# An mLSTM cell and a squared-relu FFN in one kernel: weight roundings moved one place ahead, one relu moved ahead of a conversion, four filler matmuls left out

## The chip, the core and the metric

The kernel runs on one core of one Trainium2 chip. The core has a matrix engine (PE, with its own weight-load row, PEld), a vector engine (DVE), a scalar engine (ACT), a general engine (POOL), and a queue (SP) that here only issues DMAs. Each engine runs its own list of instructions strictly in order; semaphores tie the lists together. The metric is the device time of one execution in microseconds, as the median of several runs; lower is better. Before the change five runs gave 519.08, 521.13, 518.82, 519.87 and 517.87 us, median 519.08.

## What is computed

```python
# attention: per batch and head, over 768 steps t, head_dim 40
m_new  = max(f[t] + m, i[t])
C      = exp(f[t] + m - m_new) * C + exp(i[t] - m_new) * outer(v[t], k[t])
n      = exp(f[t] + m - m_new) * n + exp(i[t] - m_new) * k[t]
y[t]   = sigmoid(o[t]) * (C @ q[t]) / max(abs(n @ q[t]), 1)
# the 8 heads side by side give x: 3072 rows of 320
h      = max(x @ w_in, 0)          # w_in  320 x 2048
out    = (h * h) @ w_out           # w_out 2048 x 320
```

All of it in fp32. The weights w_in and w_out reach the chip as pairs of 32-bit words (64-bit floats) and are turned into fp32 by the kernel itself.

## The kernel before, in words

**Tiles.** The 3072 rows of x are 24 row blocks of 128 (block s). The cell is worked in chunks: inside a block by matrix products of scores, between blocks by the carried state C. For each block: `transposes(s)` turns k and q on PE, ACT copies them out; `scores(s)` multiplies them; `weigh(s)` makes the decay weights W on ACT from the gate rows A_bc, which POOL masks first (`mask`); `weighted(s)` multiplies scores by W on DVE (tile P_sb); `attend(s)` makes three groups of matmuls, hi (from the state), dC (the state's increment) and hp (from P_sb); DVE takes them out of PSUM (num at line 466, C_sb at 471, the sum at 589); `normalise(s)` makes x_sb with six short DVE instructions (lines 595 to 603); `turn_rows(s)` turns x_sb on PE, and ACT copies it to xT. Two blocks make a group of 256 rows for the FFN: `ffn1(g, pp)` is a quarter of the first product (sixteen matmul instructions at line 649 and eight at 660 in the profile), `relu_half` the relu of a quarter on ACT (line 675, two instructions), `square_half` the squares on DVE (line 682).

**Weights.** A list of 26 pieces is rounded by class `Rounding`: pieces 0 to 9 are w_in (512 columns each), 10 to 25 are w_out (320 columns each). One piece n passes four stages: `fetch` (DMA on SP into one of four raw buffers), `words` (ACT lines 195 and 197, tiles mag and low, three buffers each), `join` (DVE lines 206, 210 and 211, then POOL line 215, which writes the fp32 weight), and `join` ends by fetching the piece four places further on, because its raw buffer is now read. `step` makes the words that are missing, usually those of one piece ahead as well, and one join. The first quarter of ffn1 needs pieces 0 to 2, the second 0 to 4, the third 0 to 7, the fourth 0 to 9.

**Order.** The order is written out by hand, and each engine takes its instructions in that order. A prologue (lines 815 to 876) treats blocks 0 and 1, with one `rounding.join()` at line 839 and three steps later on (858, 867, 876). Then a loop of eight parts, u = 0 to 7 (line 880), treats blocks 2 to 5: even parts make scores of block s = 2 + u // 2, odd parts attend to it and turn the next block's k and q; each part makes one quarter of ffn1 (u = 0 to 3: group 0). At the end of part u steps are made until `NEXT[u]` pieces are joined. After the loop a longer list of parts treats the rest, mostly ffn1, ffn2 and the turned form of the attention; its first parts join the last pieces (`LAST`).

**Buffers.** PSUM has three banks for attention products (tag at), taken in rotation by tp, scores, hi, dC and hp, and three for ffn1 (tag h_ps), also taken in rotation; `idle(n)` takes one of these too. `idle(n)` is n bf16 matmuls of zeros, 128x512, whose output nobody reads.

**DMA.** All loads go through SP's queue in program order. [...]

Of the kernel before, what the change touches and what calls it, by code (L numbers as in the profile page):

```python
# [29 lines left out]
def kernel(  # L30
# [200 lines left out]
    rounding = Rounding()  # L231
# [25 lines left out]
    def turn_gates():  # L257
        for src, dst in ((i_sb, b_T), (A_sb, eA_T)):
            tp = ps_o.tile([P, W], F32, name="tp", tag="o_ps")[:, : S // P * BH].rearrange("p (c r) -> p c r", r=BH)
            for c in range(NB):  # L260
                nc.tensor.transpose(tp[:, c, :], src[:, c * P : (c + 1) * P], ident[:BH, :BH])
            nc.scalar.activation(
                dst[:].rearrange("p b c h -> p c b h"), tp.rearrange("p c (b h) -> p c b h", b=B),
                AF.Copy if dst is b_T else AF.Exp,
            )
# [52 lines left out]
    def load_o(s):  # L318
        b, c = divmod(s, NB)
        r, (s0, s1) = next((r, (a, z)) for r, (a, z) in enumerate(RUNS) if a <= s < z)  # L320
        if s == s0:
            st["og", r] = ld.tile([P, 4, H, D], F32, name="og")
        og = st.setdefault(s, {})["og"] = st["og", r][:, s - s0]
        nc.sync.dma_start(og, o_gate[b, :, c * P : (c + 1) * P, :].rearrange("h p d -> p h d"))
# [31 lines left out]
    def mask(s):  # L356

        A = st[s]["A"][0]
        nc.gpsimd.affine_select(  # L359
            A[:], A[:], compare_op=ALU.is_ge, fill=-1e30, base=0, pattern=[[0, H], [1, P]], channel_multiplier=-1,  # L360
        )
# [9 lines left out]
    def weigh(s, masked=False, sums=True):  # L371
        b, c = divmod(s, NB)
        d = st[s]
        A, n = d["A"], H // len(d["A"])
        d["W"] = prep.tile([P, H, P], F32, name="W_sb")
        if s < X_SQ:
            d["dec"] = prep.tile([P, H], F32, name="dec")
        if len(A) == 1 and not masked:
            mask(s)
        for i in range(len(A)):  # L380
            hh = slice(i * n, (i + 1) * n)
            for h in range(n):
                nc.scalar.activation(  # L383
                    d["W"][:, i * n + h, :], A[i][:, h, :], AF.Exp, bias=b_T[:, b, c, i * n + h : i * n + h + 1],
                )
            if s < X_SQ:
                nc.scalar.activation(d["dec"][:, hh], A[i][:, :, P - 1], AF.Exp)
        if sums:
            values(s)

    def values(s):
        b, c = divmod(s, NB)
        d = st[s]
        if c + 1 < NB:
            d["vw"] = prep.tile([P, H, D1], F32, name="vw")
            nc.gpsimd.tensor_tensor(  # L396
                d["vw"][:], d["va"][:], d["W"][:, :, P - 1 : P].to_broadcast([P, H, D1]), op=ALU.mult,
            )
# [5 lines left out]
    def transposes(s, o=(False, False), apart=0):  # L404
        d = st[s]
        kqT(s)
        for i, n in enumerate(("kT", "qT")):
            if i > 0 and apart:
                idle(apart)
            tp = bank(o[i])  # L410
            for j in range(PR):
                nc.tensor.transpose(  # L412
                    tp[:, j, :], d["kq"][:, i, 2 * j : 2 * j + 2, :].rearrange("p h d -> p (h d)"), ident[:],
                )
            (nc.scalar.copy if i == 0 or s in (0, *range(2, 7)) else nc.vector.tensor_copy)(d[n], tp)

    def scores(s, o=(False, False)):
        d = st[s]

        sc = [bank(o[i]) for i in range(2)]  # L420
        for j in range(PR):
            for i in range(2):
                rows = slice(DP * i, DP * i + D)
                nc.tensor.matmul(  # L424
                    sc[i][:, j, :], lhsT=d["kT"][rows, j, :], rhs=d["qT"][rows, j, :], start=True, stop=True,
                )
        d["sc"] = sc

    def weighted(s, spare=False):
        d = st[s]  # L430
        d["P"] = []
        for i in range(2):
            t = ffn.tile([P, W], F32, name="r_sb", bufs=4) if spare else work.tile([P, W], F32, name="P_sb")
            t = t[:].rearrange("p (j t) -> p j t", j=PR)
            d["P"].append(t)
            heads = slice(i, H, 2) if s < KQ_SQ else slice(PR * i, PR * (i + 1))
            nc.vector.tensor_tensor(t, d["sc"][i], d["W"][:, heads, :], op=ALU.mult)  # L437
# [190 lines left out]
    def turn_rows(s):  # L628
        d = st[s]
        t = xT_half(s)  # L630
        tp = ps_at.tile([P, 3, P], F32, name="tp", tag="at")
        for a in range(3):
            nc.tensor.transpose(tp[:, a, :], d["x"][:, a * P : (a + 1) * P], ident[:])
        nc.scalar.copy(t, tp[:])
        del st[s]
# [29 lines left out]
    def ffn1(g, pp):  # L665
        ffn1_main(g, pp)
        ffn1_rest(g, pp, st["half"][0])

    def relu_half():
        if "half" in st:  # L670
            hs, g4 = st.pop("half")
            rs = []
            for h in hs:
                rs.append(ffn.tile([P, 2, WG], F32, name="r_sb", bufs=4))
                nc.scalar.activation(rs[-1][:], h[:], AF.Relu)  # L675
            st.setdefault("relu", []).append((rs, g4))

    def square_half():
        if st.get("relu"):
            rs, g4 = st["relu"].pop(0)  # L680
            for i, r in enumerate(rs):
                nc.vector.tensor_tensor(g4[:, :, i, :], r[:], r[:], op=ALU.mult)  # L682
# [116 lines left out]
    def idle(n):  # L799
        t = ps_h.tile([P, W], F32, name="idle", tag="h_ps")  # L800
        for _ in range(n):
            nc.tensor.matmul(  # L802
                t[:], lhsT=zeros[:, :1].to_broadcast([P, P]), rhs=zeros[:, :1].to_broadcast([P, W]), start=True, stop=True,
            )
# [32 lines left out]
    rounding.words()  # L837
    turn_gates()
    rounding.join()
    weigh(0)  # L840
    transposes(1, (False, True))
    spread_A(1)
# [33 lines left out]
    rounding.step()  # L876


    NEXT = (5, 8, 10, 11, 13, 15, 17, 19)
    for u in range(8):  # L880
        s = 2 + u // 2
        relu_half()
        if u % 2 == 0:
            if u == 0:
                ffn1(0, 0)
                scores(s)
                weighted(s)
                relu_half()
                rounding.step()
            else:  # L890
                if u == 2:
                    idle(4)
                turn_rows(s - 1)
                scores(s)
                ffn1(u // 4, u % 4)
            if u == 2:
                rounding.words()
            if u > 0:
                weighted(s)
            if u == 2:  # L900
                mask(s + 1)
                rounding.join()
                rounding.join()
                weigh(s + 1, masked=True)
                rounding.words()
            elif u == 0:
                rounding.words()
                weigh(s + 1, sums=False)
            else:
                weigh(s + 1)  # L910
                square_half()
        else:
            load_A(s + 2)
            for r in {1: (4,), 3: (5, 6), 5: (7,), 7: ()}[u]:
                load(r)
            if u == 5:
                for r in range(4, 8):
                    sigmoid(r)
            attend(s)
            if u == 3:  # L920
                square_half()
            sum_of_h(s)
            if u < 4:
                normalise(s)
            rounding.join()
            if u == 1:
                values(s + 1)
            if u > 4:
                normalise(s)
            for r in {5: (8,), 7: (9,)}.get(u, ()):  # L930
                load(r)
            for r in {5: (7,), 7: (8,)}.get(u, ()):
                pair_up(r)
            if u > 4:
                load_o(2 * s)
                load_o(2 * s + 1)
            transposes(s + 1)
            rounding.words()
            if u == 7:
                ffn1_main(1, 3)  # L940
                turn_rows(5)
                ffn1_rest(1, 3, st["half"][0])
                square_half()
                relu_half()
            else:
                ffn1(u // 4, u % 4)
                if u > 1:
                    square_half()
        if u < 4:
            load_o(4 + u)  # L950
        while rounding.done < NEXT[u]:
            rounding.step()
        if u == 1:
            square_half()
# [249 lines left out]
```

## Time and profile before

| what | value |
|---|---|
| median of five runs | 519.08 us (517.87 to 521.13) |
| the profiled execution, its own time | 519.08 us, of which the span is 517.3 us |
| PE busy | 509.2 us, 98% of the span |
| DVE busy | 335.4 us, 65%; in the stretch from 40 to 65 us of the span 4.77 to 4.93 us of each 5 |
| ACT, POOL busy | 194.2 us (38%), 91.0 us (18%) |
| granted PE clock | 0.997 as a mean; 1.00 in nearly every stretch, 0.50 from 61 to 64 us |
| PE's busy time from 65 to 120 us | 54.65 of 55 us |

The page gives busy time of each engine, its groups of instructions, and which semaphore ended each idle time; the trace gives the instructions in order of time, and stretches of the span with the busy time and the granted clock in each. The loop of eight parts runs from about 32 us (u = 0) to about 100 us; u = 1 ends at about 47 us on PE, u = 2 at about 55 us, u = 3 at about 68 us.

### The profile page before, as it was taken

The page shows a single profiled execution, that of the slowest core. Times are in us where ns is not written, and L with a number is a line of the kernel's source. Part 1 is how long each engine was busy: PE and PEld are TensorE (multiplying, and loading weights), DVE is VectorE, ACT ScalarE, POOL GpSimd, SP SyncE. Part 2 cuts the span into 40 slices and gives each one's busy share as a digit, 9 for nine tenths or more (in the row PEclk, how much of TensorE's full clock was granted, in tenths as well). Part 3 has the DMA queues.
Part 4 walks back from the last instruction along what each step waited for, and adds up shares of the span by engine and source line. Part 5 has one row for each costly group of instructions (what it writes and reads, how often), then busy time and mean ns, then how long its engine had stood idle before and what let it go on. Part 6 is the DMA issues. An engine that isn't in the chain of part 4 may idle for free.

```text
span 517.3 us, 10367 instructions
## 1 busy us (share of the span) xinstructions
PE 509.2 (98%) x3935; PEld 448.3 (87%) x3937; DVE 335.4 (65%) x638; ACT 194.2 (38%) x460; POOL 91.0 (18%) x110
## 2 busy tenths in 40 slices
PE   9998999999999999999999999999999999999997
PEld 4777788887798898998898898998998998998997
DVE  8479988877894684774864865664864863431461
ACT  3776568534455324432335424135332301103000
POOL 3255643232312120010110110111111000000000
PEclk9999899999999999999999999999999999999999
DMA  9998599976868667868676686686664221200000
GB/s 194 229 208 182 141 186 201 205 173 125 174 154 183 132 158 152 179 119 168 153 148 128 156 153 122 155 144 140 150 148 73 70 67 48 63 1 0 27 27 25
DMA packets 239394, 68.06 MB, mean 132 GB/s; under 512 B 185744, under 2 KB 233872, under 8 KB 239344
## 3 DMA queue, kind: packets, MB, share of 16 engines
q1 hardware_dynamic: 239248, 67.20, 61.4%
q8 instruction: 31, 0.51, 0.4%
q10 hardware_dynamic: 96, 0.20, 0.1%
q14 instruction: 19, 0.16, 0.1%
HBM read 55.08 MB, written 17.86 MB: 141 GB/s over the span
## 4 chain that ended last, share of the span: by engine, by line
PE 88%; DVE 4%; DMA 3%; ACT 3%; SPq 1%; issue 1%; POOL 0%; DVEq 0%; ACTq 0%; POOLq 0%
PE h_ps L743 33%; PE h_ps L649 29%; PE h_ps L660 8%; PE tp L424 3%; PE numT L534 3%; PE h_ps L689 3%; PE numT L523 2%; PE idle L802 2%; PE tp L412 1%; PE numT L512 1%; ACT W_sb L383 1%; DMA A_bc<-a_rows 1%; DMA raw<-in_moe_w_in_dram 1%; DVE mag L210 1%; PE A_ps L350 1%
## 5 line engine op out<-in xcount | busy, mean ns | idle before, releaser
L649 PE MATMUL h_ps<-xT,w_in 128*128 128x256 f32 x768 | 172.9, 382 | 2.8 <-ACT r_sb L675 1.7
L649 PEld LDWEIGHTS h_ps<-xT,w_in 128*128 128x128 f32 x768 | 144.4, 191 | 24.4 <-POOL vw L396 1.6
L675 ACT ACTIVATE r_sb<-h_ps 128x512 f32<-128x512 f32 x96 | 50.2, 598 | 108.0 <-PE h_ps L660 57.7
L743 PE MATMUL h_ps<-w_out,g 128*128 128x160 f32 x528 | 75.5, 299 | 0.0
L682 DVE TENSOR_TENSOR g<-r_sb 128x512 f32<-128x512 f32 x96 | 68.8, 767 | 10.0 <-ACT r_sb L675 10.0
L743 PEld LDWEIGHTS h_ps<-w_out,g 128*128 128x128 f32 x528 | 72.9, 190 | 0.3 <-ACT W_sb L383 0.2
L383 ACT ACTIVATE W_sb<-A_bc,b_T 128x128 f32<-128x128 f32 x176 | 53.8, 389 | 22.9 <-POOL A_bc L359 22.7
L437 DVE TENSOR_TENSOR P_sb<-tp,W_sb 128x512 f32<-128x512 f32 x46 | 29.6, 685 | 49.4 <-PE numT L534 32.9
L743 PE MATMUL h_ps<-T,S 128*128 128x160 f32 x352 | 52.3, 302 | 0.0
L743 PEld LDWEIGHTS h_ps<-T,S 128*128 128x128 f32 x352 | 48.7, 190 | 1.6 <-issue 0.9
L660 PE MATMUL h_ps<-xT,w_in 64*128 64x256 f32 x384 | 49.0, 391 | 0.0
L660 PEld LDWEIGHTS h_ps<-xT,w_in 64*128 64x128 f32 x384 | 34.8, 186 | 12.1 <-issue 9.1
L759 DVE TENSOR_TENSOR y_sb<-y_sb,h_ps 128x160 f32<-128x160 f32 x44 | 14.1, 321 | 43.4 <-PE h_ps L743 43.3
L763 ACT COPY y_sb<-h_ps 128x160 f32<-128x160 f32 x11 | 3.2, 293 | 97.9 <-PE h_ps L743 97.9
L359 POOL TENSOR_SCALAR_AFFINE_SELECT A_bc<-A_bc 128x1024 f32<-128x1024 f32 x22 | 27.0, 1226 | 69.0 <-ACT kq L369 58.2
L396 POOL TENSOR_TENSOR vw<-va,W_sb 128x328 f32<-128x328 f32 x20 | 18.9, 947 | 70.4 <-ACT W_sb L383 52.0
L490 POOL TENSOR_TENSOR Cd<-C,kq 128x164 f32<-128x164 f32 x15 | 7.0, 464 | 115.8 <-DVE C L551 100.6
L424 PEld LDWEIGHTS tp<-kqT 40*128 40x128 f32 x384 | 24.8, 188 | 2.4 <-issue 1.1
L316 DVE STREAM_TRANSPOSE kqT<-kqT 128x1024 f32<-128x1024 f32 x17 | 21.0, 1236 | 8.5 <-DMA kqT<-kq_rows 8.4
L369 ACT ACTIVATE kq<-A_bc 64x512 f32<-64x512 f32 x30 | 18.8, 628 | 19.9 <-DMA A_bc<-a_rows 18.0
L424 PE MATMUL tp<-kqT 40*128 40x128 f32 x384 | 26.1, 275 | 0.0
L743 PE MATMUL h_ps<-w_out,S 128*128 128x160 f32 x176 | 25.7, 299 | 0.0
(119 smaller groups left out, 602.6 us busy)
## 6 DMA issues: line engine op xcount, KB each, us to landing
A_bc<-a_rows SPq DMA_DIRECT2D x23, 512.0 KB, 4.9
raw<-in_moe_w_out_dram SPq DMA_DIRECT2D x16, 320.0 KB, 3.5
num_rows<-tn SPq DMA_DIRECT2D x18, 256.0 KB, 2.2
kq<-num_rows SPq DMA_DIRECT2D x72, 64.0 KB, 2.0
kqT<-kq_rows SPq DMA_DIRECT2D x34, 128.0 KB, 3.2
raw<-in_moe_w_in_dram SPq DMA_DIRECT2D x8, 512.0 KB, 4.7
kq<-in_k_dram SPq DMA_DIRECT2D x24, 160.0 KB, 4.1
va<-in_v_dram SPq DMA_DIRECT2D x24, 160.0 KB, 4.4
```

What stands on the lines that cost most here:

```text
L316: nc.vector.transpose(t, t)
L359: nc.gpsimd.affine_select(A[:], A[:], compare_op=ALU.is_ge, fill=-1e30, base=0, pattern=[[0, H], [1, P]], channel_multiplier=-1,)
L369: nc.scalar.activation(e[rows], st[s]["A"][0][rows, PR * i : PR * (i + 1), :], AF.Exp)
L383: nc.scalar.activation(d["W"][:, i * n + h, :], A[i][:, h, :], AF.Exp, bias=b_T[:, b, c, i * n + h : i * n + h + 1],)
L396: nc.gpsimd.tensor_tensor(d["vw"][:], d["va"][:], d["W"][:, :, P - 1 : P].to_broadcast([P, H, D1]), op=ALU.mult,)
L424: nc.tensor.matmul(sc[i][:, j, :], lhsT=d["kT"][rows, j, :], rhs=d["qT"][rows, j, :], start=True, stop=True,)
L437: nc.vector.tensor_tensor(t, d["sc"][i], d["W"][:, heads, :], op=ALU.mult)
L649: nc.tensor.matmul(hs[i][:, n, :], lhsT=w_in[:, a, fb * P : (fb + 1) * P], rhs=xT[:, :, a, :], start=(n == 0 and a == 0), stop=False,)
L660: nc.tensor.matmul(hs[i][:, n, :], lhsT=w_in2[rows, 2 * pp + n, :], rhs=xT[rows, :, 2, :], start=False, stop=(n == 1),)
L675: nc.scalar.activation(rs[-1][:], h[:], AF.Relu)
L682: nc.vector.tensor_tensor(g4[:, :, i, :], r[:], r[:], op=ALU.mult)
L743: nc.tensor.matmul(to, lhsT=lhsT[:, p], rhs=rhs[:, p, :], start=(start and p == 0), stop=(p == NPAIR - 1), skip_group_check=True,)
```

## The change

Five edits, no arithmetic changed:

```diff
     turn_gates()
     rounding.join()
+    rounding.join()
     weigh(0)
...
-    NEXT = (5, 8, 10, 11, 13, 15, 17, 19)
+    NEXT = (6, 9, 10, 12, 14, 16, 18, 20)
     for u in range(8):
...
             else:
-                if u == 2:
-                    idle(4)
                 turn_rows(s - 1)
...
             if u == 2:
                 mask(s + 1)
                 rounding.join()
-                rounding.join()
                 weigh(s + 1, masked=True)
-                rounding.words()
...
         if u < 4:
             load_o(4 + u)
+        if u == 1:
+            relu_half()
         while rounding.done < NEXT[u]:
             rounding.step()
```

- Piece 1 is joined in the prologue right behind piece 0, and its successor in the buffer, piece 5, is fetched there. From then on each join place of the prologue and of parts u = 0 and u = 1 treats the piece one further on, since the pieces are taken in order.
- In part u = 2 one piece (9) is joined instead of two (8 and 9), and the words of piece 10 are made by the earlier call of `words` in that part. Part u = 3 joins two pieces (10 and 11) instead of one.
- In every part from u = 3 on one more piece is done than before; the first part after the loop joins one instead of two.
- At the end of part u = 1 the relu of the second ffn1 quarter stands ahead of the words made by that part's last step; before, it stood behind them, at the head of part u = 2.
- Part u = 2 turns the rows of block 2 without the four filler matmuls ahead of it.

## The prediction

> **What bounds the kernel now.** I read the page's shares first: PE is busy 98% of the span. So only stretches where PE stands, or runs slowly, can be won, unless PE's own work falls (here by four filler matmuls). The table of waits, for PE alone in the first 180 us, lists all that is there:
>
> ```profile
> PE h_ps L649 <- ACT r_sb L675: 1.7, 2, 1.4
> ...
> PE tp L412 <- DVE num L466: 0.9, 1, 0.9
> PE h_ps L649 <- ACT xT L634: 0.6, 1, 0.6
> PE h_ps L649 <- POOL w_in L215: 0.4, 1, 0.4
> ```
>
> The places come from the timeline of PE (start, length, instruction, and in brackets the idle time before it):
>
> ```profile
> 47.23 1.04 PE L802 MATMUL idle<-zeros 128*128 128x512 bf16 x3
> 48.12 0.49 PE L633 MATMUL tp<-ident,x_sb 128*128 128x128 f32 x3
> 48.54 1.16 PE L424 MATMUL tp<-kqT 40*128 40x128 f32 x16
> 51.11 0.67 PE L649 MATMUL h_ps<-xT,w_in 128*128 128x256 f32 x2 [1.41 <-ACT r_sb L675]
> 52.17 3.29 PE L649 MATMUL h_ps<-xT,w_in 128*128 128x256 f32 x14 [0.39 <-POOL w_in L215]
> 55.39 1.13 PE L660 MATMUL h_ps<-xT,w_in 64*128 64x256 f32 x8
> 56.45 1.12 PE L446 MATMUL hi<-C_sb,kqT 128*128 128x82 f32 x8
> 57.41 1.06 PE L453 MATMUL dC<-vw,kq 128*128 128x82 f32 x8
> 58.30 1.92 PE L460 MATMUL hp<-va,P_sb 128*128 128x41 f32 x16
> 61.07 1.97 PE L412 MATMUL tp<-ident,kq 128*128 128x128 f32 x8 [0.86 <-DVE num L466]
> 62.83 4.30 PE L649 MATMUL h_ps<-xT,w_in 128*128 128x256 f32 x16
> ```
>
> The reader is to see three losses in part u = 2: the third ffn1 quarter waits for the relu of the second and then for weight piece 6; the turn of block 4 (L412) waits for a PSUM bank that num releases; and behind that the same work is slower. The last shows in the stretches of one microsecond (last three columns: granted clock, DMA share, GB/s):
>
> ```profile
> 61.00:62.00 1.00, 0.93 (x5) 0.93 (x6) 1.00 (x3) 0.00 (x0) 1.00 (x2) 0.50 0.50 46
> ```
>
> The clock stays at 0.50 to 64 us. From L412's start to L660's start it is 5.99 us here and 4.46 us one part earlier (41.71 to 46.17) and later (78.10 to 82.56): 1.53 us lost. From 65 to 120 us PE stands 0.35 us in 55. So what L412 at 61.07 gains or loses, the end gains or loses, as long as other engines keep up.
>
> **The change, part by part.** The sum is made against the profiled execution: 519.08 us, equal to the median of the runs shown, of it a span of 517.3; the 1.8 us around it stay.
>
> *Second join in the prologue.* DVE has 3.19 us idle after the first join (13.40 to 16.59); the join is 0.42 + 0.43 + 0.69 by its rows, about 2.5 when L210 must wait for POOL's add of the piece before (1.37 instead of 0.43 in such a pair at 33.16). It ends near 16.0, POOL's add near 17.4, ahead of vw at 18.11. Cost nothing; without this idle time it would cost up to 2.5.
>
> *The join that follows is not free.* The step behind attend(0) now joins piece 2 where it joined piece 1. The words of piece 1 were made at 11 us. Those of piece 2 stand in ACT's list behind a table load and two sigmoids (timeline before):
>
> ```profile
> 23.54 0.42 DVE L206 TENSOR_SCALAR mag<-mag 128x512 f32<-128x512 f32 x1
> ...
> 23.93 0.66 ACT L195 ACTIVATE mag<-raw 128x512 f32<-128x512 f32 x1
> ```
>
> mag is there at 24.59, so L206 starts 1.05 us later than 23.54, and DVE is in order: normalise(0), num, normalise(1) stand behind it (25.06 to 31.27, nearly gapless), then turn_rows(1), xT, and ffn1(0,0), which already waits 0.62 us for xT at 32.42. PE is gapless from there to 49.7. So 1.05 us passes through.
>
> *Piece 5 fetched early.* Its 512 KB (0.52 MB) go into SP's list at about 16, ahead of load(2), A_bc(2) and og(2), og(3), in a stretch that moves 171 to 244 GB/s: everything up to 33 us lands 2.1 to 3.1 us later (1.4 at the best slice, 366 GB/s). Loads of block 2 have over 5 us to spare; og's sigmoid at 31.16 just keeps its place. A_bc(2) does not: POOL's mask waited 0.17 us for it at 26.67. It would land at 28.0 to 29.5, against POOL free at 27.6 after the delayed add, so mask, Cd and the C add (1.13, 0.73, 0.88) slide onto normalise(1). What such a collision costs is in the trace: normalise(2) under the same three POOL instructions took 3.8 us (42.45 to 46.25), normalise(1) 2.2. Bounds: 0.7 won, if mask lands so late that normalise(0) escapes it, against 0.75 lost. Replaying both landings gives 0.4 to 0.75 lost; I take 0.45. Front delay F = 1.05 + 0.45 = 1.5 (0.4 to 1.8).
>
> *Joins one piece ahead.* Piece 6 now stands where piece 5 stood: POOL's add at 47.91 to 49.22 instead of 50.73 to 52.11, plus F. Piece 7 takes the next place (ends 52.1 + F), piece 8 the third. Words and raw buffers stay as far ahead as before, and piece 9's fetch moves from 47.90 to about 41, so the 0.71 us that ACT waited for it at 52.53 goes; ACT was not the bound there.
>
> *Relu ahead of words, no zeros.* The relu waited behind words whose mag buffer came free at 49.25. Now it starts when L660 of the quarter ends, about 48.2 + F. The four zeros (0.87 us) go, and also the bank they took: the next quarter's first bank is then the free one, and the relu is needed for the second only. The xT copy of block 2 goes behind the words (50.5 + F); it frees the bank of hi, wanted at 53.75 + F. Free.
>
> So PE: L660 ends 47.30, turn and scores to 48.95, the quarter starts there, its second pair of matmuls at 49.43 wants piece 6 (49.22): no wait. Quarter 48.95 to 52.67 (3.72), rest to 53.75, hi to 54.75; all plus F. **What is late next is DVE.** It runs three joins in a row from 46.16, then
>
> ```profile
> 53.05 2.36 DVE L682 TENSOR_TENSOR g<-r_sb 128x512 f32<-128x512 f32 x2
> 55.33 1.27 DVE L437 TENSOR_TENSOR P_sb<-tp,W_sb 128x512 f32<-128x512 f32 x2
> ```
>
> None of this moves forward. dC's bank is that of the first score half, released at 56.0 by P_sb; then dC 0.9, hp 1.8: hp ends at 58.7 + F. PE stands 1.25 us in between.
>
> *One join less in u = 2.* DVE's pair 56.53 to 60.61 becomes one join, 1.5 us, and num ends at 58.53 instead of 61.02; the bank is free before hp ends. L412 starts at 58.7 + F instead of 61.07. **Gain 2.37 - F = 0.87.**
>
> *One join more in u = 3.* It goes between squares and P_sb(4) (L437 at 69.80): 1.2 us by the rows at 66.32 to 67.53, up to 2.1 with POOL's mask on it. hp(4) wants P_sb at 76.35, DVE gave it at 71.1. num(4) then ends at 75.0 + F; with L412 of the next part at 78.10 - 0.87 that is in time, but a lead of over 3.1 - F there is not kept. Later parts do the same joins under other piece numbers; the first part after the loop is relieved of one.
>
> **A rule weighed.** The half clock is worth as much as the rest. The Trainium skill, TensorE: Matmul & The Clock Gate, section "Why this matters for your kernels", asks only that there be no PE gaps over some 3 us between bursts. By the rule the gaps to come (0.7 to 1.6) are harmless and the removed zeros guarded nothing: the clock would be full, and the gain 3.1 - F = 1.6. The row speaks otherwise: half clock came at 60.9 behind a gap of 0.86 us and hp's short matmuls (41 columns). The changed kernel has hi, 1.25 us of nothing, dC and hp in a row at the same place. I follow the row: the half clock stays, 1.53 us as before. In no run shown so far does the clock's timing repeat or vary, so that is a choice.
>
> **Forecast: 519.08 - 0.87 = 518.2 us**, its own range 517.4 to 519.2. Chance 0.42.
>
> **Rivals.**
> - *Full clock in u = 3.* For: the rule, and other hp stretches that keep 1.00. Against: the gap only moves. L412 ends 1.53 sooner, then num(4) at 75.0 + F takes over: gain 3.1 - F = 1.6 with F = 1.5, 2.0 with F = 1.05: 517.3. Chance 0.28. The two are told apart at 1.56 us.
> - *Slower: the front breaks the clock.* Place: 28 to 34 us. Now PE stands 0.2 and 0.6 us there, with two fours of zeros between the turns. With F = 1.8 the gaps grow to about 1.0 before turn_rows(0), 1.0 before turn_rows(1) and 0.6 before ffn1(0,0); if the clock halves at 33 for 3.2 us, ffn1(0,0) loses 1.5. Then 2.37 - 1.8 - 1.5 = 0.9 slower, 520.0; a second half-clock stretch, behind the 1.25 us gap or where the four zeros stood, makes it 521.5. It decides as soon as front delay and halving together exceed 2.4. Against: F need not be that large, and a gap of 1.41 at 51 left the clock at 1.00. Chance 0.22, most of it beyond +0.3%, because unnamed collisions of DVE and POOL (each up to 0.9 by L210's rows) add on this side.
> - *Nothing.* The earlier L412 is eaten at num(4), or a late transfer holds words or A_bc(4): 519.1. Chance 0.08.
>
> **Numbers.** I call under 0.3% (1.56 us) no change, since runs of one kernel spread by that much (517.87 to 521.13). Faster is the second case and a slice of the first: 0.30. Slower is most of the third: 0.20. The rest, 0.50, is no change. Range 516.0 to 520.9: the low end is F = 0.4 with a full clock (2.7 to 3.1), the high end the third case with part of a second halving.
>
> **What would show it.** Right: L206 at 24.6 and ffn1(0,0) starting near 33.9; no waits of line 649 in u = 2 on the relu or on w_in; PE idle before dC of about 1.2 us, released by P_sb; L412 of block 4 near 60.2. Wrong: A_bc(2) landing before 27.6 (F = 1.05), half clock near 33, num still last before L412, or a new wait in u = 4 on num.

## The result, and the profile after

The changed kernel takes 521.43 us (median of 26 runs, 519.94 to 525.0); the kernel before, on the same chip, 518.82 us (47 runs). The ratio is 1.0052, with a 95% interval of 1.004 to 1.0064: 0.5% slower, where 518.2 us had been forecast and 520.9 was the upper end of the range. The profiled execution took 521.78 us, of it a span of 520.0, with a mean granted clock of 0.99 instead of 0.997.

The table of waits of the changed kernel, PE alone, first 180 us (total, times, longest):

```profile
PE dC L453 <- DVE P_sb L437: 1.4, 1, 1.4
PE idle L802 <- DVE zeros L797: 0.9, 1, 0.9
PE hp L460 <- PE dC L453: 0.8, 1, 0.8
PE h_ps L649 <- ACT xT L634: 0.6, 1, 0.6
PE numT L534 <- DVE P_sb L437: 0.5, 1, 0.5
PE h_ps L649 <- ACT r_sb L675: 0.3, 1, 0.3
```

The three waits that the change was followed through (relu, w_in, num ahead of L412) are gone from u = 2, and the wait for P_sb ahead of dC stands there as forecast (1.25 expected). What was not forecast is the line `hp L460 <- PE dC L453`. The dC that it names had ended at 25.60; hp's bank is the one that normalise(0) reads last at L601, on DVE:

```profile
23.86 0.43 DVE L206 TENSOR_SCALAR mag<-mag 128x512 f32<-128x512 f32 x1 [0.99 <-ACT mag L195]
...
25.90 0.44 DVE L601 TENSOR_TENSOR x_sb<-hp,og 128x320 f32<-128x320 f32 x1
```

L601 ends at 26.34, and hp starts at 26.44. The timeline of PE has both new gaps, at the front and in u = 3:

```profile
23.60 1.10 PE L446 MATMUL hi<-C_sb,kqT 128*128 128x82 f32 x8
...
26.44 1.95 PE L460 MATMUL hp<-va,r_sb 128*128 128x41 f32 x16 [0.84 <-PE dC L453]
28.22 0.60 PE L633 MATMUL tp<-ident,x_sb 128*128 128x128 f32 x3
29.04 1.49 PE L802 MATMUL idle<-zeros 128*128 128x512 bf16 x3 [0.22 <-issue]
30.32 1.84 PE L412 MATMUL tp<-ident,kq 128*128 128x128 f32 x8
31.99 1.03 PE L802 MATMUL idle<-zeros 128*128 128x512 bf16 x4
32.87 0.49 PE L633 MATMUL tp<-ident,x_sb 128*128 128x128 f32 x3
33.93 3.72 PE L649 MATMUL h_ps<-xT,w_in 128*128 128x256 f32 x16 [0.57 <-ACT xT L634]
...
54.01 1.13 PE L660 MATMUL h_ps<-xT,w_in 64*128 64x256 f32 x8
55.07 1.12 PE L446 MATMUL hi<-C_sb,kqT 128*128 128x82 f32 x8
57.58 1.12 PE L453 MATMUL dC<-vw,kq 128*128 128x82 f32 x8 [1.39 <-DVE P_sb L437]
58.53 2.88 PE L460 MATMUL hp<-va,P_sb 128*128 128x41 f32 x16
61.21 1.95 PE L412 MATMUL tp<-ident,kq 128*128 128x128 f32 x8
62.95 5.17 PE L649 MATMUL h_ps<-xT,w_in 128*128 128x256 f32 x16
68.05 1.13 PE L660 MATMUL h_ps<-xT,w_in 64*128 64x256 f32 x8
```

The kernel before, at the places that the prediction did not show:

```profile
24.36 1.10 PE L446 MATMUL hi<-C_sb,kqT 128*128 128x82 f32 x8
...
29.57 1.03 PE L412 MATMUL tp<-ident,kq 128*128 128x128 f32 x8
...
32.42 3.72 PE L649 MATMUL h_ps<-xT,w_in 128*128 128x256 f32 x16 [0.62 <-ACT xT L634]
...
67.06 1.14 PE L660 MATMUL h_ps<-xT,w_in 64*128 64x256 f32 x8
```

To be read in the second column: L412 takes 1.84 us at 30 instead of 1.03 before; in u = 3 hp takes 2.88 instead of 1.92 and L649 takes 5.17 where it took 4.30 before and takes 3.7 elsewhere. No wait stands ahead of them. The stretches of one microsecond give the reason (third column from the right: granted clock):

```profile
29.00:30.00 1.00, 0.96 (x3) 0.40 (x3) 0.97 (x2) 0.33 (x1) 1.00 (x2) 0.50 0.84 290
30.00:31.00 1.00, 1.00 (x6) 0.80 (x5) 0.96 (x3) 0.00 (x0) 0.92 (x2) 0.50 1.09 297
...
59.00:60.00 1.00, 1.00 (x8) 1.00 (x7) 1.00 (x3) 1.00 (x5) 0.21 (x1) 0.63 0.00 0
60.00:61.00 1.00, 1.00 (x6) 1.00 (x6) 1.00 (x3) 1.00 (x5) 1.00 (x1) 0.50 0.36 56
...
65.00:66.00 1.00, 1.00 (x4) 0.73 (x3) 0.93 (x4) 0.33 (x1) 0.00 (x0) 0.50 1.20 197
66.00:67.00 1.00, 1.00 (x6) 0.90 (x5) 0.96 (x3) 0.00 (x0) 0.34 (x1) 0.96 1.05 109
```

The clock is 0.50 from about 28.5 to 32 and again from 59.3 to 66.1. What the slices lack of 1.00 adds up to 1.71 us at the front and 3.41 us in u = 3; before it was 1.71 us in all (60.8 to 64.2 us).

**Where the 2.7 us of span came from.** Starts of the same PE instructions, before and after: first quarter of ffn1, L660, 36.07 and 37.58 (+1.51); third quarter 55.39 and 54.01 (-1.38); fourth quarter 67.06 and 68.05 (+0.99); first matmul of ffn2 120.04 and 121.10 (+1.06); L660 near 161, 160.33 and 162.33 (+2.00); end +2.7. So u = 2 won 2.9 us, u = 3 lost 2.4, the front lost 1.5, and 1.7 more went after 120 us.

### The profile page after: what moved, and what is told of

Same layout as the page of the kernel before. It is cut to its first block, busy times and chain, and to the rows that moved or that the text cites. A ratio compares the mean times of both kernels' runs of the same rounds, so it can differ in the third digit from the quotient of the medians.

```text
span 520.0 us, 10358 instructions
## 1 busy us (share of the span) xinstructions
PE 511.2 (98%) x3932; PEld 450.2 (87%) x3933; DVE 335.9 (65%) x638; ACT 193.7 (37%) x460; POOL 91.9 (18%) x110
## 4 chain that ended last, share of the span: by engine, by line
PE 74%; DVE 2%; issue 2%; DMA 1%; ACT 1%; SPq 0%; DVEq 0%
PE h_ps L743 31%; PE h_ps L649 24%; PE h_ps L660 7%; PE numT L534 3%; PE tp L424 3%; PE h_ps L689 3%; PE numT L523 2%; PE numT L512 1%; DMA kq<-in_k_dram 1%; DVE g L682 0%; DVE mag L210 0%; DMA kq<-num_rows 0%; DMA num_rows<-tn 0%; ACT W_sb L383 0%; DVE tn L545 0%
## 5 line engine op out<-in xcount | busy, mean ns | idle before, releaser
L649 PE MATMUL h_ps<-xT,w_in 128*128 128x256 f32 x768 | 173.7, 384 | 1.7 <-ACT xT L634 0.6
L649 PEld LDWEIGHTS h_ps<-xT,w_in 128*128 128x128 f32 x768 | 144.9, 192 | 23.8 <-issue 1.4
L660 PE MATMUL h_ps<-xT,w_in 64*128 64x256 f32 x384 | 49.0, 391 | 0.0
L660 PEld LDWEIGHTS h_ps<-xT,w_in 64*128 64x128 f32 x384 | 34.8, 186 | 12.1 <-issue 8.8
L743 PE MATMUL h_ps<-T,g 128*128 128x160 f32 x176 | 25.7, 299 | 0.0
```

Of the source, the lines that this page charges most:

```text
L649: nc.tensor.matmul(hs[i][:, n, :], lhsT=w_in[:, a, fb * P : (fb + 1) * P], rhs=xT[:, :, a, :], start=(n == 0 and a == 0), stop=False,)
L660: nc.tensor.matmul(hs[i][:, n, :], lhsT=w_in2[rows, 2 * pp + n, :], rhs=xT[rows, :, 2, :], start=False, stop=(n == 1),)
L743: nc.tensor.matmul(to, lhsT=lhsT[:, p], rhs=rhs[:, p, :], start=(start and p == 0), stop=(p == NPAIR - 1), skip_group_check=True,)
```

## The experiments

Two theories stood against each other. **CLOCK**: the new gaps in PE's work, 0.84 us ahead of hp of block 1 and 1.39 us ahead of dC of block 3, are what halves the clock behind them, and that halving is the loss. **FRONT**: the loss is the delay of DVE at the front (late words, early fetch), and the clock is an accident. Zeros that nobody reads fill a gap and take no wait away, so they separate the two; moving the words takes a wait away. `fill(n)` below is n bf16 matmuls of zeros, 128x512, into a bank that is free there. Each ratio is to executions of the kernel before that were taken together with that kernel; the median of the kernel before lay between 518.82 and 520.06 us in the four such sets, so ratios are to be compared across experiments, not microseconds.

### Zeros in the gap ahead of dC

```diff
+        if s == 3:
+            fill(6)
         dC = ...
```

> The changed kernel with six zero matmuls (1.3 us) between hi and dC of block 3, in the gap of 1.39 us where dC waits for P_sb; they write a bank that nobody uses. CLOCK: no stretch at 0.50 from 59.4 to 66; hp takes 1.9 instead of 2.9 us, the fourth ffn1 quarter 3.7 instead of 5.2; 2.4 us less at L660 of that quarter, of which DVE's num of block 4 lets 2 or so through: 519.4 (ratio to before 1.001). FRONT: the clock is a bystander, PE waits for others either way: 521.4, as the changed kernel.

Measured: 520.2 us (22 runs), ratio 1.0019 (1.0004 to 1.0035). In its profile hp of block 3 takes 1.92 us and L649 behind it 3.62, while the half clock at the front, 28 to 31 us, is still there. By ratio 0.33% of the 0.52% comes back, so the gap in u = 3 was the larger part of the loss.

### Words of attend(0) ahead of the sigmoid

```diff
     load_o(3)
+    rounding.words()
     sigmoid(0)
```

> The changed kernel with the words of piece 2 made ahead of the two first sigmoids, so that its join need not wait for ACT. FRONT: the join starts about 1 us earlier, x of block 0 too, the gap before hp(1) of 0.84 us goes, ffn1(0,0) starts 0.5 to 1.5 us earlier and the total falls by as much: 520.0 to 520.9. CLOCK: the halving behind hp(1) (28.8 to 32.0) may go with the gap, but the one at 59.4 stays whatever the front does: not below 520.4, and unchanged if A_bc(2), landing at 28.4, sets the front.

Measured: 519.7 us (14 runs), ratio 1.0007 (0.998 to 1.0034). The first gap closes; ffn1(0,0) starts at 31.29 us instead of 33.93 (7.98 us behind the start of hi of block 1, instead of 10.33):

```profile
25.14 1.92 PE L460 MATMUL hp<-va,r_sb 128*128 128x41 f32 x16
26.88 0.53 PE L633 MATMUL tp<-ident,x_sb 128*128 128x128 f32 x3
```

POOL's mask waited 3.80 us for A_bc(2) in this profile, until 29.32, and so missed normalise(1). The gap ahead of dC is still there (1.38 us), and in this execution the clock stayed at 1.0 behind it: a gap need not be followed by a halving in each execution. The gain fits both theories: a wait is gone, and so is a gap.

### Both

```diff
     load_o(3)
+    rounding.words()
     sigmoid(0)
...
+        if s == 3:
+            fill(6)
```

> The changed kernel with both the words of piece 2 ahead of the first sigmoids and six zero matmuls between hi and dC of block 3. CLOCK: both gaps behind which it halved are gone or filled; nearly all executions near the full clock, where the run with early words alone had 516.6 us: 516.5 to 517.5, ratio to before 0.997. FRONT: words early alone had 519.7 in the median and the zeros in the later gap add nothing: 519.5 to 520.

Measured: 517.68 us (22 runs), ratio 0.9963 (0.9947 to 0.9978). This beats both kernels, by 0.4% the one before and by 0.9% (1.0052 against 0.9963) the changed one. The clock is 1.0 in its profile. Since one wait went as well as both gaps, this run alone does not separate the theories.

### Two fills, and no wait taken away

```diff
+        if s == 1:
+            fill(4)
         hp = ...
...
+        if s == 3:
+            fill(6)
         dC = ...
```

> The changed kernel, words late as they are, with zeros in both gaps: four ahead of hp of block 1 (gap of 0.84 us) and six between hi and dC of block 3. No wait is taken away. CLOCK: the clock stays full in most executions and the total falls by what the half clock cost, 518.0 to 519.0 against 521.4. FRONT: DVE's late join and all behind it stay, so ffn1(0,0) stays near 33.9 and the total at 520.2, as with the later gap filled alone, or above.

Measured: 519.5 us (14 runs), ratio 0.9996 (0.9979 to 1.0013). This is the run that separates the theories. The words are as late as in the changed kernel, the waits are there, ten matmuls of zeros are added, and by ratio 0.56% comes back. Its 519.5 us is above the 518.0 to 519.0 expected by CLOCK, but the kernel before was slower in this set too; its interval ends below the 1.0019 of the kernel with the later gap filled alone, which FRONT expected, though that ratio has an interval of its own (1.0004 to 1.0035). Its timeline of PE:

```profile
26.50 1.03 PE L813 MATMUL fill<-zeros 128*128 128x512 bf16 x4
27.50 1.95 PE L464 MATMUL hp<-va,r_sb 128*128 128x41 f32 x16
...
55.53 1.47 PE L813 MATMUL fill<-zeros 128*128 128x512 bf16 x6
57.07 1.12 PE L455 MATMUL dC<-vw,kq 128*128 128x82 f32 x8
58.03 1.92 PE L464 MATMUL hp<-va,P_sb 128*128 128x41 f32 x16
59.77 1.07 PE L412 MATMUL tp<-ident,kq 128*128 128x128 f32 x8
60.68 3.62 PE L653 MATMUL h_ps<-xT,w_in 128*128 128x256 f32 x16
```

hp, L412 and the quarter behind them have their full-clock lengths (1.92, 1.07, 3.62) at the place where the changed kernel had 2.88, 1.95, 5.17.

That does not make every wait free. Words early with the later gap filled, taken in the same set, is 1.8 us faster (517.68 against 519.5), and the clock accounts for some 0.3 us of it (0.14 and 0.36 halvings by the count given below, at 1.5 us each). On PE's way from hi of block 1 to L660 of the fourth quarter the two profiles are alike (39.71 and 39.56 us), so the difference is not the late words there. The profile with two fills starts hi of block 1 0.96 us later and has a wait of 1.21 us for kq near 191 us that the other has not; whether that holds in all executions is open.

### The gap ahead of L412 of block 4, in the kernel before

```diff
+            if u == 3:
+                fill(4)
             transposes(s + 1)
```

> The kernel before with four zero matmuls in its own gap of 0.86 us, ahead of the turn of block 4 that waits for num. CLOCK: the stretch at 0.50 from 61 to 64 goes in most executions; where it went by itself before, the median was 518.3 against 519.5: 518.3, ratio 0.999. FRONT: says nothing here, 519.2.

Measured: 519.84 us (14 runs), ratio 0.9996 (0.9979 to 1.0013). From 56 to 68 us the clock is 1.00; in the profiled execution a halved stretch lies at 52 to 55 us instead, behind the relu and w_in waits. Over all executions halvings are rarer (0.21 per execution against 0.90 of the kernel before in the same set, by the count given below), and yet the median shows no gain: CLOCK's 0.999 is neither met nor excluded. Executions without a halving took 519.55 us here (11 of them) and 518.62 in the kernel before (12), so about 0.9 us is lost elsewhere. The profile names a wait of 0.94 us of L649 for kq near 193 us, which the kernel before has not; whether the filler brings it is not shown.

### The early fetch taken back

```diff
-    rounding.join()
+    rounding.join(fetch=False)
...
     load_o(3)
+    rounding.fetch()
     sigmoid(0)
```

> The changed kernel with piece 5 fetched behind the loads of block 2 (k, q, v, A_bc, o) instead of ahead of them. FRONT: A_bc(2) lands near 26.7 again, POOL's mask no longer stands on normalise(1), ffn1(0,0) up to 0.75 us earlier: 520.7 to 521.4. CLOCK: the same for the front, 59.4 to 66 unchanged; so alone this run tells what the early fetch costs, from 0 to 0.8 us.

Measured: 522.08 us (6 runs), ratio 1.0062 (1.0039 to 1.0085), as slow as the changed kernel. Nothing waits for A_bc(2) any more, and ffn1(0,0) starts at 34.89 us, later still. POOL's row for the mask in this kernel, and in the changed one:

```profile
27.30 1.35 POOL L360 TENSOR_SCALAR_AFFINE_SELECT A_bc<-A_bc 128x1024 f32<-128x1024 f32 x1
```

```profile
28.43 1.09 POOL L359 TENSOR_SCALAR_AFFINE_SELECT A_bc<-A_bc 128x1024 f32<-128x1024 f32 x1 [1.53 <-DMA A_bc<-a_rows]
```

So nothing was won by the later fetch; with six runs a cost of the early fetch of some tenths of a microsecond is not excluded. Nor is the wait of 1.53 us for A_bc surely its work: the kernel before with a filler, which has no early fetch, shows one of 1.95 us at the same place.

### Zeros of u = 2 put back

```diff
+                if u == 2:
+                    idle(4)
                 turn_rows(s - 1)
```

> The changed kernel with the four zero matmuls of part u = 2 put back. CLOCK: they end at 49 us, ten before the clock falls, and dC waits for P_sb at 57.5 all the same, 0.87 us of it now covered (gap 1.39 to about 0.5): the halving at 59.4 comes less often, 520 to 521; nothing is lost, since PE waits for DVE there. ZEROS (a third theory: leaving out the zeros is what let the clock fall): back to 518.8 or below. FRONT: 521.4.

Measured: 521.03 us (14 runs), ratio 1.0017 (0.9992 to 1.0043), executions from 517.19 to 524.11. The gap ahead of dC is 0.59 us here. This is an inconclusive middle: the clock was 1.0 in some executions and 0.987 in others, and the interval excludes neither CLOCK nor ZEROS. That the four zeros are not needed for a full clock is shown by the kernels with filled gaps above, which leave them out.

### Relu ahead and zeros out, without the shift of the roundings

```diff
         if u < 4:
             load_o(4 + u)
+        if u == 1:
+            relu_half()
...
-                if u == 2:
-                    idle(4)
```

> The kernel before with only the relu ahead of the words and without the four zeros; the roundings stay where they were. Theory CLOCK (the changed kernel loses by half-clock stretches that follow gaps on PE beside short matmuls): PE reaches the third ffn1 quarter some 2 us earlier but piece 6 is still written at 52.1, so a gap of about 2.3 us opens at 49.5 to 52; nothing is won by 52.2, and 1.5 us are lost if the clock halves behind it: 518.8 to 520.3. Theory FRONT (it loses by the delay that the second join in the prologue brings: words late, A_bc(2) late): no front delay here, ffn1(0,0) at 32.4 as before, so 518.8 or a little less, and no stretch at 0.50 beyond that of 61 to 64.

Measured: 519.3 us (22 runs), ratio 1.001 (0.9995 to 1.0025). In the kernel before, these two edits alone change nothing that the runs tell apart; the w_in wait grows to 2.19 us and eats what they give. Behind that wait the profile has a stretch of half clock, from 51.9 to 55.3 us, as CLOCK had it and FRONT had not.

### Relu back behind the words

```diff
         if u < 4:
             load_o(4 + u)
-        if u == 1:
-            relu_half()
```

> The changed kernel with the relu back behind the words. CLOCK and FRONT agree: without the filler matmuls the first half of the matmuls of that step needs no relu, and the relu of the second half ends some 0.4 us before it is needed, so nothing changes: 521.4 us, ratio 1.004 to 1.006, granted clock about 0.99. Rival (the relu's move is what the lead hangs on): TensorE waits for it and the time is 0.3 us or more longer, ratio above 1.006; or the words, now sooner on ScalarE, shorten the gap before dC of block 3 and the time falls to 520.5 us or below, ratio under 1.003.

Measured: 521.24 us (22 runs), ratio 1.0026 (1.0007 to 1.0045): between "nothing changes" and the second rival, which had expected under 1.003, and the interval reaches 1.0045. PE waits 0.21 us for the relu inside the quarter, so hi comes later and the gap ahead of dC is 0.91 us instead of 1.39. This kernel also spreads most: 517.92 to 525.28 us.

### Squares moved, so that no gap is left

```diff
     load_o(3)
+    rounding.words()
     sigmoid(0)
...
             attend(s)
             if u == 3:
+                square_half()
                 square_half()
...
             rounding.step()
-        if u == 1:
-            square_half()
```

> The changed kernel with the words of attend(0) written ahead of the sigmoid (as in words early), and with the squares of the second relu half of u=1 put behind attend(3)'s num and C_sb on VectorE, so that P_sb(3) comes some 1.3 us sooner and no wait of TensorE stands between hi and dC of block 3; no zeros are added. CLOCK: both gaps behind which the clock halved are gone because the waits are gone, so the granted clock is as with words early and the six zeros (0.997 to 1.0), hp of block 3 takes 1.92 us and L649 behind it about 3.7 us; 516.5 to 518.5 us, ratio 0.995 to 0.998. Rival (the lead is VectorE's to give): P_sb comes sooner but num, C_sb and the squares behind it come as late or later, TensorE waits for num at the tp of block 4 or for the squares at ffn2, and the time is that of words early alone, 519.7 us, ratio 1.000 to 1.002.

Measured: 518.29 us (14 runs), ratio 0.9977 (0.9963 to 0.9991). The time is what CLOCK expected, and the wait for num that the rival named is there as well. PE now runs from L649 at 48.68 to L660 at 61.62 us without a gap and at a clock of 1.00, and L412 comes at 57.14 us, 3.9 us ahead of the kernel before. But then:

```profile
61.62 1.14 PE L660 MATMUL h_ps<-xT,w_in 64*128 64x256 f32 x8
64.31 0.52 PE L633 MATMUL tp<-ident,x_sb 128*128 128x128 f32 x3 [1.56 <-DVE x_sb L602]
```

```profile
57.00 0.49 DVE L471 TENSOR_TENSOR C_sb<-dC,bdm 128x328 f32<-128x328 f32 x1
57.41 4.82 DVE L682 TENSOR_TENSOR g<-r_sb 128x512 f32<-128x512 f32 x4
62.15 0.48 DVE L589 TENSOR_TENSOR num<-num,hp 128x328 f32<-128x328 f32 x1
```

POOL works beside them from 56.8 to 61.7 us, and DVE's four squares take 1.2 us each (as the two in the kernel before, 2.36 us together at 53.05), against a median of 0.68 us of all squares of this kernel; normalise(3) stands behind them. PE gives 1.56 us back at x_sb and 1.06 us at num(4) near 75 us, and behind that second gap, from 75.4 to 78.8 us, the profile has its one stretch of half clock. The reordering closes one gap and opens two others behind it.

### What the granted clock of all executions says

Each execution lists its mean granted clock, and the values come in steps: 1.0, 0.997, 0.993, 0.990, 0.987, 0.984. One step is 0.0033 of 518 us = 1.71 us, just what one halved stretch lacks in the profiles above (3.4 us at 0.50). So (1 - clock) x 518 / 1.71, rounded, estimates the halvings of an execution:

| kernel | gap ahead of hp(1) | gap ahead of dC(3) | executions | halvings, mean | ratio to before |
|---|---|---|---|---|---|
| before | none | none (0.86 ahead of L412) | 137 | 0.87 | 1 |
| before, L412 gap filled | none | none | 14 | 0.21 | 0.9996 |
| changed | 0.84 | 1.39 | 27 | 2.93 | 1.0052 |
| changed, fetch late | 0.84 | 1.38 | 6 | 2.83 | 1.0062 |
| changed, relu back | 0.84 | 0.91 | 22 | 2.14 | 1.0026 |
| changed, zeros of u = 2 back | 0.84 | 0.59 | 14 | 1.86 | 1.0017 |
| changed, dC gap filled | 0.84 | filled | 22 | 1.50 | 1.0019 |
| changed, words early | none | 1.38 | 14 | 1.43 | 1.0007 |
| changed, both filled | filled | filled | 14 | 0.36 | 0.9996 |
| changed, words early, dC gap filled | none | filled | 22 | 0.14 | 0.9963 |
| changed, words early, squares moved | none | none (1.56 and 1.06 later) | 14 | 0.64 | 0.9977 |
| before, relu ahead, no zeros | none | none (2.19 ahead of L649) | 22 | 1.45 | 1.001 |

No execution of the changed kernel had fewer than two halvings (8 had two, 16 three, 3 five). Within one kernel the time rises with the count: with the relu back, 518.91 us at none (3 executions), 518.60 at one (6), 521.56 at three (9), 524.93 at five (2); with the words early, 516.63 at none (5) and 520.10 at two (7). A straight line through time against count gives 1.2 us per halving for the changed kernel, 1.3 with the relu back, 1.5 with the zeros back and 2.0 with the words early (0.7 to 1.1 in the kernel before). From before to after there are 2.06 more of them: at 1.2 to 1.5 us each an estimate of 2.5 to 3.1 us, against 2.6 us measured. Either gap alone leaves about 1.45 of them; without both 0.14 to 0.64 are left.

## Why the prediction was wrong, step by step

- **Second join in the prologue.** No new wait of PE ahead of 24 us: right. The first zeros took 4.59 us in this execution and 5.30 in the one before, so all positions at the front are to be read against hi of block 1 (23.60 and 24.36), not against zero.
- **Late join of piece 2.** Right in size: L206 at 23.86 with 0.99 us of waiting for the words (1.05 forecast). But the step "1.05 us passes through" to xT was followed along DVE only. The bank that hp(1) wants is held until normalise(0) has read it, as the rows of DVE above show, so the wait also opened 0.84 us ahead of hp(1), and this gap is in no step of the prediction; its third case had "about 1.0 before turn_rows(0)", which is the same delay seen one product later.
- **Early fetch, 0.45 us.** Not shown to be a cost of the fetch. Mask, Cd and the add of C did land on normalise(1), but with the fetch later they land there in part too (mask at 27.30 us) and the kernel is as slow.
- **F = 1.5.** Measured 1.51 (33.93 against 32.42), which is luck. Counted from hi of block 1, ffn1(0,0) came 10.33 us behind it, against 8.06 before: 2.27 us later. Three kernels with the same late words whose profiles keep the full clock there show the delay alone: 1.09 us with the zeros back, 1.14 with the relu back, 0.71 with both gaps filled. So 0.7 to 1.1 us is the delay and the rest, 1.1 to 1.6 us, is half clock at the front, which the forecast's main case put at nothing; a start that was 0.76 us earlier hid half of that.
- **Joins one piece ahead, relu ahead, zeros out.** The two waits of L649 in u = 2 went, L660 of the third quarter starts at 54.01 against 54.2 forecast (52.67 + 1.5), and P_sb ends the gap ahead of dC, 1.39 us against 1.25. Right.
- **"The half clock stays, 1.53 us as before."** This is the step that failed: the half clock was entered as one stretch before and after, and became three (1.71 us lacking of full clock before, 1.71 at the front and 3.41 in u = 3 after). L412 came at 61.21 us instead of 60.2: of that 1.0 us, 0.96 is hp at half clock. Behind it L649 lost 0.87 us more than before. Together 1.83 us, against 1.86 us between the forecast (-0.87) and the result (+0.99) at L660 of the fourth quarter. The prediction weighed "full" against "as before" for this place and put "twice" only into the slower case; there the mechanism, with its chance of 0.22, is the one that happened. That its 521.5 us is also the time measured is partly luck, since 1.7 us of the loss came behind 120 us, which that case did not have.
- **The rule weighed.** Gaps of 0.84 and 1.39 us were followed by half clock here, and filling them made it rare (2.93 to 0.36 halvings). The Trainium skill, TensorE: Matmul & The Clock Gate, section "Why this matters for your kernels", asks for no PE gaps over some 3 us, and by it the time would have been 517.5 us; the measurement decides. Part 1 of the same page, "The HAM clock gate", gives the gate two levels and a window of some 3.4 us that runs freely, independent of the kernel. The levels 1.00 and 0.50, stretches of 3.4 us, and their shifting from execution to execution agree with it. The choice of "row over rule" was right in direction, but a row of one execution tells that a place can halve the clock, not how often or for how long. The row was also read a little wrong: by its slices the clock fell at 60.8 us, inside the gap (60.2 to 61.07) and not behind it.
- **"What L412 gains or loses, the end gains or loses."** Failed as well. After 120 us the changed kernel loses another 1.7 us, and its waits name 1.3 of it: numT for P_sb (0.52), L649 for xT (0.24) and, near 195 us, L649 for kq from DRAM (0.55). The P_sb wait is in the profile of every kernel with the shifted roundings (0.34 to 0.73) and at most 0.20 in the others, so it belongs to the shift; why P_sb is late there was not tried. The kq wait comes and goes, also in the kernel before with a filler (0.94). A lead is capped as well: with two fills L660 near 64 us is 2.8 us ahead of before, and num(4) takes 0.57 of it (forecast: a lead over 3.1 - F is not kept), P_sb 0.73, kq 1.21. Its span is again 517.3.

**What the change is worth without the clock.** Three profiles let it be estimated. From hi of block 1 to L660 of the fourth quarter the kernel before takes 42.70 us, of which 1.53 is half clock. The same way takes 39.94 us with the zeros back and 40.01 with the relu back, at full clock (rows of the first):

```profile
24.16 1.10 PE L446 MATMUL hi<-C_sb,kqT 128*128 128x82 f32 x8
...
33.31 3.72 PE L649 MATMUL h_ps<-xT,w_in 128*128 128x256 f32 x16 [0.57 <-ACT xT L634]
...
64.10 1.14 PE L660 MATMUL h_ps<-xT,w_in 64*128 64x256 f32 x8
...
75.82 1.09 PE L412 MATMUL tp<-ident,kq 128*128 128x128 f32 x8 [0.57 <-DVE num L466]
```

So at equal clock the change is about 1.2 us ahead there, as the sum has it with the delay measured (2.37 - 1.1); with both gaps filled it is 1.6 (2.37 - 0.7). At the next L412 the wait for num(4) has left 0.5 us (51.66 and 51.72 against 52.21 us behind hi, the 1.53 taken off), and the wait for P_sb near 124 us takes 0.3 to 0.4 more. In executions with no halving, the kernels built on the changed one that keep the late words take 517.69 to 519.33 us in the median (3 to 9 executions each), the kernel before 518.33 to 518.62. A gain at the end is therefore not shown; the 0.5% is, within what these estimates can tell, the clock.

## What to carry to other kernels

When a change moves a wait on PE, look at the granted clock behind the new gap: here gaps of 0.84 and 1.39 us, among matmuls of 41 and 82 columns and transposes, were followed by half clock for 3.4 and 6.8 us, and in u = 3 that cost more than the gap. Whether the short matmuls matter was not tried. Read the granted clock of many executions, not of one profile, before taking it as given. A few matmuls of zeros in the gap are a cheap test, and when they bring the time back with all waits in place, the clock was the larger cost. They are no sure cure: in the kernel before they made halvings rarer and the time no shorter.

## What was not expected of the hardware

- The granted clock drops to 0.50 behind gaps of 0.8 to 1.4 us, for 3.4 us, and in u = 3 for 6.8 us, two stretches on end. How large a gap must be is not settled, and a gap is neither enough nor needed. The waits of 1.41 and 0.39 us ahead of L649 left the clock at 1.00 in the kernel before, while in the kernel before with a filler the same two waits ended in half clock from 52.0 us. With gaps of 0.84 and 0.91 us (relu back) the profile showed full clock at both places, while 11 of 22 executions of that kernel had three or more halvings. The one halved stretch in that profile, 14.6 to 18.0 us, has no gap ahead of it: PE is busy 1.00 of each microsecond from 10 us on, just ahead with twelve transposes of 32x32.
- The clock does not fall at once. In these profiles it fell between 0.3 us before the end of a gap (before, 60.8 against 61.07) and 2.6 us behind it (fetch late, 29.5 against 26.90).
- The start is not the same in each execution (first zeros 4.59 and 5.30 us), and hi of block 1 starts at 23.60 and 24.36 us.
- Whether POOL's mask falls onto normalise(1) varies from profile to profile over the same instructions: with the words early it came at 29.32 us and ffn1(0,0) started 6.15 us after hp(1); in the kernel with words early and zeros, the same up to there, at 28.19 us, with PE waiting 1.06 us for x_sb, and 7.07 us after hp(1).
